# Hedgehog linear attention and an ELU layer on one core: loads by batch, weights in pieces, 64-row tail matmuls, and another order of steps

## The chip, the cores and the metric

One core of one Trainium2 chip. Its engines run their own instruction streams and wait for each other through semaphores: TensorE (PE, matmuls; PEld is its weight load), VectorE (DVE), ScalarE (ACT), GpSimd (POOL), and SyncE (SP), which only issues transfers. POOL issues transfers too: those go on a queue that software fills (`q0 software_dynamic`) and can change the type on the way; SyncE's queue (`q1 hardware_dynamic`) copies as it is. The metric is the device time of one launch in microseconds.

## What is computed

Inputs: q, k, v of shape (batch 8, heads 8, rows 576, 64), w_phi (64, 128), moe_w_in (512, 2048), moe_w_out (2048, 512), all float32; the output is (4608, 512) float32.

```python
def phi(x):
    proj = np.einsum('bhsd,df->bhsf', x, w_phi)
    proj = proj - np.max(np.abs(proj), axis=-1, keepdims=True)
    return np.concatenate([np.exp(proj), np.exp(-proj)], axis=-1)
q_p, k_p = phi(q), phi(k)
kv = np.einsum('bhsf,bhsd->bhfd', k_p, v)
z = np.sum(k_p, axis=2)
num = np.einsum('bhsf,bhfd->bhsd', q_p, kv)
den = np.einsum('bhsf,bhf->bhs', q_p, z)[..., None] + 1e-06
x = (num / den) put back to (4608, 512): a row per token, heads side by side
h = x @ w_in
g = np.where(h > 0.0, h, np.exp(np.minimum(h, 0.0)) - 1.0)
out = g @ w_out
```

## The kernel before

**Quads.** The attention runs in 16 *quads* of four heads, two per batch (`attention_steps`, L154). A head has 576 rows: 512 *main* rows, four to a partition, and a *tail* of 64 rows. Two heads share a 128-row transpose, so a quad has eight main tiles and one tail tile, in which partitions 0 to 63 hold the tails of the even heads (s = 0) and 64 to 127 those of the odd heads (s = 1).

The steps of a quad: `transposes` brings k and q into the layout that the projections need (L166, L174; evicted by VectorE). `k_head` (five: four heads and the tails) projects (L195), takes the maximum of absolute values on VectorE (L202) and two exponentials on ScalarE (L215) into EK. The maximum isn't subtracted: `k_scale` forms exp(-m) and exp(m) (em, L223) and multiplies them into v on POOL (vs, L229, and the tails vst, L240); a column of ones beside v gives z. `q_head` does projection and maximum for q; `q_features` makes the projection the other way round (L250) with its exponentials (L258); `kv` sums EK against vs (L288 tails, L299 main); `out_head` multiplies the features of q with kv (L322) and joins the two halves on VectorE (L331, L337), `out_tail` does so for the tails (L344 to L360); `divide` takes 1/den on VectorE (L367 to L373) and multiplies on POOL (x, L376 and L382); `x_out` transposes x (L393, L405) into xT, the input of the second part.

**MoE units.** Tokens come in nine chunks of 512: chunk b holds the main rows of batch b, the ninth all tails. A first-product unit `mm1(ch, jt)` is four matmuls (L438), an exponential on ScalarE (e_sb), a subtraction on POOL (u_sb, L448) and the select on VectorE (gT, L451); a chunk has 16. A second-product unit `mm2(ch, tt)` is sixteen matmuls (L459), a copy on ScalarE and a store from SyncE; a chunk has four. That makes 180 units.

**Order.** Slot n (n = 0 to 16) holds kv, out and x of quad n-1 and transposes of quad n+1 beside the projections of quad n, by a list written out in `slot_steps` (L483). In the list the transposes of x (`old["x"]`) stand after the q heads and before the q features. Between the steps come MoE units: chunk b is released after slot 2b+2 and its 20 units are spread over the next two slots (L534 to L557); 136 units are placed in slots 3 to 16, 44 follow. The text's order is not quite the order on the engines: the framework plans each engine's stream with costs of its own and may move an instruction ahead of others that it expects to wait.

**Loads.** k and q go through POOL's queue, cast to bf16, per quad (`load_quad`, L131); the tails per batch in six transfers (`load_tails`, L104) into tiles that keep all batches; v through SyncE, one transfer a head, into rows of 65 floats that hold the column of ones. w_in comes in eight transfers before slot 0, w_out in four after slot 1. All PSUM tiles of the attention share four buffers, those of the MoE four others.

Of the kernel before, what the change touches and what calls it, by code (L numbers as in the profile page):

```python
# [8 lines left out]
FP32 = mybir.dt.float32  # L9
# [3 lines left out]
ACT = mybir.ActivationFunctionType  # L13

# [7 lines left out]
def kernel(  # L22
# [10 lines left out]
    nc = tc.nc  # L33
# [12 lines left out]
    N_CHUNK = NTOK // CHUNK  # L46
    NT = 4
    MAIN = NT * P
# [5 lines left out]
    loads = ctx.enter_context(tc.tile_pool(name="loads", bufs=3))  # L54
    work = ctx.enter_context(tc.tile_pool(name="work", bufs=2))
    small = ctx.enter_context(tc.tile_pool(name="small", bufs=4))
    xtp = ctx.enter_context(tc.tile_pool(name="xtp", bufs=3))
# [10 lines left out]
    make_identity(nc, ident)  # L68

    w_phi_both = consts.tile([P, 2, F], BF16)  # L70
    nc.vector.memset(w_phi_both, 0.0)
    nc.gpsimd.dma_start(out=w_phi_both[0:D, 0, :], in_=w_phi)
    nc.gpsimd.dma_start(out=w_phi_both[D:P, 1, :], in_=w_phi)
# [7 lines left out]
    def load_w_in():  # L81
        for ct in range(N_CT):
            for c in range(2):
                nc.gpsimd.dma_start(
                    out=w_in_sb[c * D:(c + 1) * D, ct, :],
                    in_=w_in_r[ct // 2, c, ct % 2],
                )

    def load_w_out():
        for jt in range(0, N_JT, 4):  # L90
            nc.gpsimd.dma_start(
                out=w_out_sb[:, jt:jt + 4, :], in_=w_out_r[:, jt:jt + 4, :]
            )
# [5 lines left out]
    q_tails = consts.tile([P, NQ, 2, D], BF16)  # L99
    k_tails = consts.tile([P, NQ, 2, D], BF16)  # L100
    v_tails = consts.tile([P, NQ, 2, D1], BF16)
    nc.vector.memset(v_tails[:, :, :, D:D1], 1.0)

    def load_tails(b):  # L104
        for src, dst in ((k, k_tails), (q, q_tails), (v, v_tails)):
            heads = src[b].rearrange("(gc s) j d -> s j gc d", s=2)
            for s in range(2):
                nc.gpsimd.dma_start(
                    out=dst[s * TAIL:(s + 1) * TAIL, 2 * b:2 * b + 2, :, 0:D].rearrange(
                        "p g c d -> p (g c) d"  # L110
                    ),
                    in_=heads[s, MAIN:S],
                )


    NV = 3
    v_bufs = []
    for i in range(NV):
        vb = consts.tile([P, 4, NT, D1], FP32, name=f"v_main{i}")
        nc.vector.memset(vb[:, :, :, D:D1], 1.0)  # L120
        v_bufs.append(vb)

    vst_bufs = []
    for i in range(2):
        t = consts.tile([P, 2, 2, 2, D1], BF16, name=f"vst{i}")
        nc.vector.memset(t, 0.0)
        vst_bufs.append(t)

    qk_loaded = {}

    def load_quad(i):  # L131
        b, qd = divmod(i, 2)
        got = []
        for src, nm in ((k, "k_main"), (q, "q_main")):
            t = loads.tile([P, 4, NT * D], BF16, name=nm)
            nc.gpsimd.dma_start(  # L136
                out=t,
                in_=src[b, 4 * qd:4 * qd + 4, 0:MAIN, :].rearrange(
                    "h (p t) d -> p h (t d)", t=NT
                ),  # L140
            )
            got.append(t)
        vb = v_bufs[i % NV]
        for hh in range(4):
            nc.sync.dma_start(
                out=vb[:, hh, :, 0:D],
                in_=v[b, 4 * qd + hh, 0:MAIN, :].rearrange(
                    "(p t) d -> p t d", t=NT
                ),
            )  # L150
        qk_loaded[i] = (got[0], got[1], vb)


    def attention_steps(i):  # L154
# [3 lines left out]
        def transposes():  # L158
            k_main, q_main, _ = qk_loaded[i]
            kT = work.tile([P, 9, P], BF16, name="kT")  # L160
            qT = work.tile([P, 9, P], BF16, name="qT")
            for src, dst in ((k_main, kT), (q_main, qT)):
                tr = apsum.tile([P, 8, P], BF16, name="tr", tag="ap")
                for hh in range(4):
                    for tp in range(2):
                        nc.tensor.transpose(  # L166
                            tr[:, 2 * hh + tp, :],
                            src[:, hh, tp * P:(tp + 1) * P],
                            ident,
                        )  # L170
                nc.vector.tensor_copy(dst[:, 0:8, :], tr)  # L171
            trt = apsum.tile([P, 2, P], BF16, name="trt", tag="ap")
            for n, (src, dst) in enumerate(((k_tails, kT), (q_tails, qT))):
                nc.tensor.transpose(  # L174
                    trt[:, n, :],
                    src[:, i, :, :].rearrange("p c d -> p (c d)"),
                    ident,
                )
            nc.vector.tensor_copy(kT[:, 8, :], trt[:, 0, :])
            nc.vector.tensor_copy(qT[:, 8, :], trt[:, 1, :])  # L180
            st["kT"], st["qT"] = kT, qT
            st["m_k"] = small.tile([P, 18], FP32, name="m_k")
            st["m_q"] = small.tile([P, 18], FP32, name="m_q")
            st["EK"] = work.tile([P, 4, 2, NT * F], BF16, name="EK")
            st["EKt"] = work.tile([P, 2, 2 * F], BF16, name="EKt")
            st["Eq"] = work.tile([P, 2, 2, 2, 4 * P], BF16, name="Eq")
            st["Eqt"] = work.tile([P, 2, 2 * P], BF16, name="Eqt")

        def project(xT, hh, m):
# [4 lines left out]
            for j in range(n):  # L194
                nc.tensor.matmul(  # L195
                    pk[:, 2 * j:2 * j + 2, :].rearrange("p a b -> p (a b)"),
                    xT[:, 2 * hh + j, :],
                    w_phi_rhs,
                    start=True,
                    stop=True,  # L200
                )
            nc.vector.tensor_reduce(  # L202
                m[:, 4 * hh:4 * hh + 2 * n],
# [16 lines left out]
        def k_scale():  # L220
            em = small.tile([P, 2, 18], FP32, name="em")
# [4 lines left out]
            vb = qk_loaded[i][2]  # L226
            vs = work.tile([P, 4, 2, NT, D1], BF16, name="vs")
            for hh in range(4):
                nc.gpsimd.tensor_tensor(  # L229
                    vs[:, hh],  # L230
                    vb[:, hh:hh + 1].to_broadcast((P, 2, NT, D1)),
                    em[:, :, 4 * hh:4 * hh + 4, None].to_broadcast(
                        (P, 2, NT, D1)
                    ),
                    op=ALU.mult,
                )
            vst = vst_bufs[i % 2]
            for s in range(2):
                r = slice(s * TAIL, (s + 1) * TAIL)
                nc.gpsimd.tensor_tensor(  # L240
                    vst[r, :, :, s, :],
                    v_tails[r, i:i + 1].to_broadcast((TAIL, 2, 2, D1)),
                    em[r, :, 16:18, None].to_broadcast((TAIL, 2, 2, D1)),
                    op=ALU.mult,
                )
# [209 lines left out]
    def mm2(ch, tt):  # L455
# [15 lines left out]
        else:  # L471
            for e in range(2):
# [4 lines left out]
                )  # L477

    def slot_steps(n):  # L483
# [104 lines left out]
```

## Time and profile before

| | us |
|---|---|
| median of 3 runs (lowest, highest) | 509.34 (508.05, 510.24) |
| the profiled execution | 507.1 |
| its span in the trace | 505.3 |
| TensorE busy | 409.6 |
| VectorE, POOL, ScalarE busy | 306.1, 278.5, 268.3 |

The span is from the first to the last instruction in the trace. A busy share is an average over stages with different limits; rows of the profile name line, engine, operation, output <- input, shape and count, then busy time and mean length, then the idle time just before and what ended it.

### The profile page before, as it was taken

How to read it: one execution, taken by the hardware profiler on the slowest of the kernel's cores; microseconds unless marked ns; L12 is line 12 of the kernel's file. 1: busy time of each engine (PE TensorE's matmuls, PEld its weight loads, DVE VectorE, ACT ScalarE, POOL GpSimd, SP SyncE). 2: the span in 40 equal slices, each digit the busy share in tenths (PEclk: the TensorE clock that was granted, in tenths of full speed). 3: DMA queues.
4: the chain of work that ended last, by engine and by line, in shares of the span. 5: the costliest groups of instructions: out<-in, count | busy, mean ns of one | idle time of the engine just before them, and what ended most of it. 6: DMA issues, size and time to landing. Idle time of an engine off the chain costs nothing.

```text
span 505.3 us, 8410 instructions
## 1 busy us (share of the span) xinstructions
PE 409.6 (81%) x3070; PEld 223.1 (44%) x3120; DVE 306.1 (61%) x647; ACT 268.3 (53%) x581; POOL 278.5 (55%) x420
## 2 busy tenths in 40 slices
PE   2573727495979797979797979797979798999996
PEld 1251415252635364536363546354545354444442
DVE  2562826886857677766777577757775855334420
ACT  1742608292847474847484748474847462444431
POOL 8669799747473737373737383818281734333310
PEclk9965959797989899989999999999998999899999
DMA  9999948231323232324242424200000000110113
GB/s 157 212 181 198 116 61 76 47 43 43 44 63 64 62 64 64 64 64 64 64 64 62 64 65 64 62 22 21 22 23 23 21 22 22 42 43 21 43 52 72
DMA packets 71944, 32.55 MB, mean 64 GB/s; under 512 B 48352, under 2 KB 66784, under 8 KB 71904
## 3 DMA queue, kind: packets, MB, share of 16 engines
q0 software_dynamic: 32864, 14.19, 23.1%
q1 hardware_dynamic: 39040, 17.83, 13.2%
q8 instruction: 24, 0.39, 0.3%
q14 instruction: 16, 0.13, 0.1%
HBM read 36.77 MB, written 9.44 MB: 91 GB/s over the span
## 4 chain that ended last, share of the span: by engine, by line
PE 52%; POOL 20%; DVE 13%; DMA 6%; issue 4%; ACT 4%; POOLq 0%; ACTq 0%
PE po L459 22%; PE ph L438 13%; POOL x L376 7%; DMA q_main<-in_q_dram 5%; POOL vs L229 4%; DVE m_q L202 4%; PE pq L250 4%; PE pn L322 3%; PE pkv L299 2%; POOL vst L240 2%; PE pk L195 2%; ACT EK L215 2%; POOL u_sb L448 2%; PE tr L166 2%; DVE den L367 2%
## 5 line engine op out<-in xcount | busy, mean ns | idle before, releaser
L448 POOL TENSOR_SCALAR u_sb<-e_sb 128x512 bf16<-128x512 f32 x144 | 88.9, 623 | 134.9 <-ACT e_sb L446 129.5
L459 PE MATMUL po<-w_out_sb,gT 128*128 128x512 bf16 x559 | 148.1, 389 | 1.8 <-DVE gT L451 1.4
L451 DVE SCALAR_TENSOR_TENSOR gT<-u_sb,ph 128x512 bf16<-128x512 bf16 x144 | 97.9, 683 | 78.9 <-POOL u_sb L448 78.1
L438 PE MATMUL ph<-xT,w_in_sb 128*128 128x512 bf16 x480 | 131.0, 390 | 4.6 <-DVE gT L451 3.4
L446 ACT ACTIVATE e_sb<-ph 128x512 f32<-128x512 f32 x144 | 87.3, 611 | 48.8 <-PE ph L438 46.8
L258 ACT ACTIVATE Eq<-pq 128x512 bf16<-128x512 f32 x128 | 65.2, 616 | 54.7 <-PE pq L250 54.7
L459 PEld LDWEIGHTS <-gT 128*128 128x128 bf16 x576 | 54.4, 100 | 50.5 <-issue 4.6
L438 PEld LDWEIGHTS <-w_in_sb 128*128 128x128 bf16 x576 | 54.6, 100 | 49.6 <-issue 6.8
L215 ACT ACTIVATE EK<-pk 128x512 bf16<-128x512 f32 x128 | 69.4, 612 | 13.1 <-DVE m_k L202 13.0
L229 POOL TENSOR_TENSOR vs<-v_main,em 128x520 bf16<-128x520 f32 x64 | 65.7, 1063 | 17.9 <-ACT em L223 17.7
L202 DVE TENSOR_REDUCE m_k<-pk 128x4 f32<-128x512 f32 (+1 forms) x80 | 50.4, 632 | 25.9 <-PE pk L195 25.6
L467 ACT COPY o_sb<-po 128x512 f32<-128x512 f32 x36 | 21.2, 589 | 68.0 <-PE po L459 67.5
L393 PE MATMUL tr<-ident,x 128*128 128x128 bf16 x128 | 14.6, 248 | 52.7 <-POOL x L376 52.7
L202 DVE TENSOR_REDUCE m_q<-pk 128x4 f32<-128x512 f32 (+1 forms) x80 | 48.5, 628 | 1.3 <-PE pk L195 0.5
L322 PEld LDWEIGHTS <-Eq 128*128 128x128 bf16 x512 | 28.9, 98 | 24.9 <-issue 17.0
L376 POOL TENSOR_TENSOR x<-tot,rec 128x256 bf16<-128x256 f32 x64 | 37.2, 614 | 3.1 <-DVE rec L373 3.0
L393 PEld LDWEIGHTS <-x 128*128 128x128 bf16 x128 | 8.4, 108 | 68.8 <-POOL x L376 68.8
L322 PE MATMUL pn<-kv,Eq 128*128 128x65 bf16 x512 | 34.0, 194 | 3.8 <-ACT EK L215 2.6
L195 PE MATMUL pk<-w_phi_both,qT 128*128 128x256 bf16 x144 | 29.6, 292 | 8.4 <-DVE m_q L202 7.0
L136 POOL DMA_DIRECT2D k_main<-in_k_dram x16 | 12.8, 802 | 35.9 <-PE tr L166 25.3
L195 PE MATMUL pk<-w_phi_both,kT 128*128 128x256 bf16 x144 | 29.6, 284 | 3.3 <-ACT EK L215 1.0
L171 DVE COPY kT<-tr 128x1024 bf16<-128x1024 bf16 x16 | 11.1, 692 | 34.1 <-PE tr L166 34.1
(61 smaller groups left out, 462.2 us busy)
## 6 DMA issues: line engine op xcount, KB each, us to landing
v_main<-in_v_dram SPq DMA_DIRECT2D x64, 128.0 KB, 3.3
out_dram<-o_sb SPq DMA_DIRECT2D x32, 256.0 KB, 2.6
k_main<-in_k_dram POOLq DMA_DIRECT2D x16, 256.0 KB, 5.3
q_main<-in_q_dram POOLq DMA_DIRECT2D x16, 256.0 KB, 5.7
w_in_sb<-in_moe_w_in_dram POOLq DMA_DIRECT2D x8, 256.0 KB, 10.2
w_out_sb<-in_moe_w_out_dram POOLq DMA_DIRECT2D x4, 512.0 KB, 8.3
out_dram<-o_sb SPq DMA_DIRECT2D x8, 128.0 KB, 2.3
k_tails<-in_k_dram POOLq DMA_DIRECT2D x16, 32.0 KB, 2.8
```

Source lines behind the costliest of these rows:

```text
L195: nc.tensor.matmul(pk[:, 2 * j:2 * j + 2, :].rearrange("p a b -> p (a b)"), xT[:, 2 * hh + j, :], w_phi_rhs, start=True, stop=True,)
L202: nc.vector.tensor_reduce(m[:, 4 * hh:4 * hh + 2 * n], pk[:, 0:2 * n, :], axis=AX.X, op=ALU.max, apply_absolute_value=True,)
L215: nc.scalar.activation(dst, pk, ACT.Exp, scale=1.0 - 2.0 * sg)
L229: nc.gpsimd.tensor_tensor(vs[:, hh], vb[:, hh:hh + 1].to_broadcast((P, 2, NT, D1)), em[:, :, 4 * hh:4 * hh + 4, None].to_broadcast((P, 2, ...
L258: nc.scalar.activation(st["Eq"][:, par, c, sg, :], pq, ACT.Exp, scale=1.0 - 2.0 * sg)
L322: nc.tensor.matmul(pt[:, t, :], st["Eq"][:, par, c, sg, o:o + P], st["kv"][:, c, s, sg, :], start=True, stop=True,)
L376: nc.gpsimd.tensor_tensor(st["x"][:, s, :, c, :], st["tot"][:, hh, :, 0:D], rec[:, 4 * hh:4 * hh + 4, None].to_broadcast((P, NT, D)), op=A ...
L438: nc.tensor.matmul(ph, w_in_sb[:, ct, jt * P:(jt + 1) * P], xTs[ch][:, ct, :], start=(ct == 0), stop=(ct == N_CT - 1),)
L446: nc.scalar.activation(e_sb, ph, ACT.Exp)
L448: nc.gpsimd.tensor_scalar(u_sb, e_sb, -1.0, 1.0, op0=ALU.add, op1=ALU.mult)
L451: nc.vector.scalar_tensor_tensor(gTs[ch][:, jt, :], u_sb, 0.0, ph, op0=ALU.min, op1=ALU.max)
L459: nc.tensor.matmul(po, gT[:, jt, tt * P:(tt + 1) * P], w_out_sb[:, jt, :], start=(jt == 0), stop=(jt == N_JT - 1),)
```

## The change

- **Loads.** One tile a batch and tensor holds mains and tails (`stage`, two buffers). k and q go by batch in one main and two tail transfers each on POOL's queue (batch 0 by halves), v on SyncE, float32 and contiguous by 1 KB pieces, w_phi on SyncE with a cast on VectorE. There is no column of ones in v: a POOL copy puts em into vs.
- **Weights.** w_in in eight and w_out in eight transfers, issued one after each step of slots 0 and 1, with batch 1's k and q between them. v of batch 1 waits for a memset that stands behind `k_scale` of quad 0.
- **Layout.** The 18 columns of a quad are kept as two heads of nine, so that main and tail share one tile: vs in four products of 128 x 512 and two of 128 x 128, x in two of 128 x 576, and one `den`.
- **Tail matmuls.** `kv` now takes one s at a time and its tails as four matmuls over 64 partitions (rows r); `out_tail` as eight with 64 weight columns into one PSUM tile.
- **Order.** In a slot `x_out` stands last, after q features and transposes; `k_scale` stands before the last two out heads, and q heads between these. Slot 2 does quad 1's kv, out and x first. MoE units run by a rate, 136 over slots 2.5 to 17, and first products are preferred until four have run.

```diff
     def load_main(eng, n, b, h0, h1):
+        eng.dma_start(
+            out=kqv[b][n][:, h0 * HW:h1 * HW].rearrange("p (h n) -> p h n", n=HW),
+            in_=(k, q, v)[n][b, h0:h1, 0:MAIN, :].rearrange(
+                "h (p t) d -> p h (t d)", t=NT
...
         def k_scale():
-            for hh in range(4):
+            vs = st["vs"] = work.tile([P, 2, 2 * NS, D1], BF16, name="vs")
+            nc.gpsimd.tensor_copy(vs[:, :, :, D], em)
+            for c in range(2):
+                for sg in range(2):
+                    r = slice(c * NS, c * NS + 2 * NT)
+                    o = (4 * qd + 2 * c) * HW
+                    nc.gpsimd.tensor_tensor(
+                        vs[:, sg, r, 0:D],
+                        vb[:, o:o + 2 * HW].rearrange("p (n d) -> p n d", d=D),
+                        em[:, sg, r, None].to_broadcast((P, 2 * NT, D)),
...
+        def kv(s):
...
+            r = slice(s * TAIL, (s + 1) * TAIL)
+            for c in range(2):
+                for sg in range(2):
+                    nc.tensor.matmul(
+                        pkv[:, c, sg, :],
+                        st["EKt"][r, sg, c * F:(c + 1) * F],
+                        st["vs"][r, sg, c * NS + 8, :],
...
         def out_tail():
+            pt = apsum.tile([P, 2, 2, D1], FP32, name="pnt", tag="ap")
             for s in range(2):
                 r = slice(s * TAIL, (s + 1) * TAIL)
+                for sg in range(2):
+                    for c in range(2):
+                        o = c * P + s * TAIL
+                        nc.tensor.matmul(
+                            pt[r, sg, c, :],
+                            st["Eqt"][:, sg, o:o + TAIL],
+                            st["kv"][:, s, c, sg, :],
...
+    def moe_unit():
+        if second and (not first or run[0] >= N_JT // 4):
+            mm2(*second.pop(0))
+            run[0] = 0
+            return
+        ch, jt = first.pop(0)
+        mm1(ch, jt)
+        run[0] += 1
+        if jt == N_JT - 1:
+            second.extend((ch, tt) for tt in range(CHUNK // P))
...
+        if n == 2:
+            return (
+                old["kv"] + old["out"] + old["x"]
+                + [lambda: chunk_ready(0)]
+                + new["k"] + new["scale"] + new["q"] + new["qf"] + nxt["tr"]
+            )
...
+        steps = (
+            old["kv"][:1] + kk[:1] + old["kv"][1:] + kk[1:3]
+            + old["out"][:1] + kk[3:4] + old["out"][1:2] + kk[4:]
+            + (new or none)["scale"]
+            + old["out"][2:3] + qq[:1] + old["out"][3:4] + qq[1:2]
+            + old["out"][4:] + qq[2:] + (new or none)["qf"]
+        )
+        if nxt:
+            steps += nxt["tr"]
+        steps += old["x"]
+        if n % 2 == 0:
+            steps.append(lambda: chunk_ready(n // 2 - 1))
...
+    def load_v(b, gate=False):
+        if gate:
+            nc.vector.memset(kqv[b][2][:, 0:1], 0.0)
+        load_main(nc.sync, 2, b, 0, 8)
+        load_tails(nc.sync, 2, b)
...
+    UNITS = 136
...
+        if n % 2 == 0 and 1 < n // 2 + 1 < B:
+            alloc_batch(n // 2 + 1)
+            extra += load_kq(n // 2 + 1)
+            load_v(n // 2 + 1)
         steps = slot_steps(n)
         for j, step in enumerate(steps):
             step()
+            if n == 0 and step is quads[0]["scale"][0]:
+                load_v(1, gate=True)
+            if extra and (n < 2 or j % 3 == 2):
+                extra.pop(0)()
+            due = (n + (j + 1) / len(steps) - 2.5) * UNITS / 14.5
+            while done < due and (first or second):
+                moe_unit()
```

Also, `xtp` has two buffers for three, and `o_sb` two for four.

More of the change, by code (lines that the diff above doesn't have):

```diff
@@ L45 @@
     CHUNK = 512
-    N_CHUNK = NTOK // CHUNK
     NT = 4
+    NS = 9
     MAIN = NT * P
@@ L116 @@
[L116 to L139, printed above, removed]
+    HW = NT * D
@@ L156, in attention_steps @@
         st = {}
[L158 to L187, printed above, removed]
```

369 lines of the change are left out of this document (166 added, 203 removed).

## The prediction

> **What bounds the kernel now.** I began with the page's busy shares and slices.
>
> ```profile
> PE 409.6 (81%) x3070; PEld 223.1 (44%) x3120; DVE 306.1 (61%) x647; ACT 268.3 (53%) x581; POOL 278.5 (55%) x420
> PE   2573727495979797979797979797979798999996
> ...
> PE 52%; POOL 20%; DVE 13%; DMA 6%; issue 4%; ACT 4%; POOLq 0%; ACTq 0%
> PE po L459 22%; PE ph L438 13%; POOL x L376 7%; DMA q_main<-in_q_dram 5%; POOL vs L229 4%; DVE m_q L202 4%; PE pq L250 4%; PE pn L322 3%; PE pkv L299 2%; POOL vst L240 2%; PE pk L195 2%; ACT EK L215 2%; POOL u_sb L448 2%; PE tr L166 2%; DVE den L367 2%
> ```
>
> The average misleads: TensorE is slack in the first fifth, alternates 9 and 7 in the middle and is full at the end. In the chain of waits TensorE has half, but POOL's x and vs come next. So I cut the span where the key transposes of a slot end, and asked for the busy time of each stretch: slots 0, 1 and 2, then slots 6 to 15 in one, slot 16, and what follows it (columns: start:end, length, then busy us of PE, PEld, DVE, ACT, POOL, the granted clock, DMA share, GB/s).
>
> ```profile
> 0.00:21.90 21.90, 10.12 (x60) 6.09 (x60) 9.47 (x22) 9.76 (x21) 15.28 (x29) 1.00 1.15 180
> 21.90:51.70 29.80, 14.85 (x120) 9.34 (x120) 12.15 (x30) 10.58 (x27) 24.45 (x35) 0.60 1.27 192
> 51.70:78.40 26.70, 13.72 (x131) 8.39 (x130) 12.81 (x31) 10.53 (x25) 23.61 (x36) 0.68 0.85 81
> ...
> 152.50:410.00 257.50, 229.09 (x1831) 126.85 (x1860) 181.01 (x389) 159.36 (x350) 138.69 (x204) 0.97 0.24 50
> 410.00:429.60 19.60, 17.13 (x143) 9.17 (x145) 11.67 (x26) 7.37 (x16) 7.63 (x13) 1.00 0.07 28
> 429.60:505.30 75.70, 70.62 (x315) 31.67 (x319) 22.11 (x34) 26.71 (x45) 19.77 (x32) 0.97 0.14 46
> ```
>
> Slots 1 and 2 hold no MoE matmuls worth the name, yet take 29.8 and 26.7 us with POOL busy 24. Ten later slots take 25.75 us each, TensorE busy 22.91 of them (VectorE 18.1, ScalarE 15.9, POOL 13.9). What ends TensorE's idle 2.84 us there is nearly one thing (view of waits for TensorE, 152.5 to 410 us: total us, times, longest):
>
> ```profile
> PE tr L393 <- POOL x L376: 24.6, 20, 2.8
> ```
>
> 2.46 us a slot: the transposes of x stand ahead of the q features, and POOL delivers x late. The middle is TensorE plus one wait. The start is another matter. POOL in order of time (start, length, engine, line; in brackets the idle time before it and what ended it):
>
> ```profile
> 20.20 0.76 POOL L136 DMA_DIRECT2D q_main<-in_q_dram  x1 [0.61 <-DMA w_in_sb<-in_moe_w_in_dram]
> 20.97 4.09 POOL L229 TENSOR_TENSOR vs<-v_main,em 128x520 bf16<-128x520 f32 x4
> 25.04 1.31 POOL L240 TENSOR_TENSOR vst<-v_tails,em 64x260 bf16<-64x260 bf16 x2
> ...
> 34.64 0.75 POOL L91 DMA_DIRECT2D w_out_sb<-in_moe_w_out_dram  x1 [1.50 <-DMA k_main<-in_k_dram]
> 38.44 4.09 POOL L229 TENSOR_TENSOR vs<-v_main,em 128x520 bf16<-128x520 f32 x4
> ```
>
> ```profile
> 11.51 1.44 PE L195 MATMUL pk<-w_phi_both,kT 128*128 128x256 bf16 x6
> ...
> 26.39 0.38 PE L288 MATMUL pkv<-vst,EKt 128*128 128x130 bf16 x2 [4.39 <-POOL vst L240]
> 46.42 1.18 PE L393 MATMUL tr<-ident,x 128*128 128x128 bf16 x8 [8.44 <-POOL x L376]
> ```
>
> POOL issues loads between its products and stops at some of them until an earlier transfer has landed; counted in order of issue, it is each time the one eight before. The work behind then reaches TensorE late: 4.39 and 8.44 us. The order of issue is the planner's, not the text's: the tail loads, written after slots 0 to 12, are all out by 88 us.
>
> ```profile
> L108 POOL DMA_DIRECT2D v_tails<-in_v_dram x16: 610/642/689, 7.4 to 88.0; - x16
> ```
>
> **The change, part by part.** *x last.* The 2.46 us go if POOL's x is done in time. The new slot has 26 steps, scale is the 10th and x the 26th, so in a slot of 23 us 14.2 us lie between. POOL's work in them:
>
> ```profile
> L229 POOL TENSOR_TENSOR vs<-v_main,em 128x520 bf16<-128x520 f32 x64 | 65.7, 1063 | 17.9 <-ACT em L223 17.7
> L376 POOL TENSOR_TENSOR x<-tot,rec 128x256 bf16<-128x256 f32 x64 | 37.2, 614 | 3.1 <-DVE rec L373 3.0
> L382 POOL TENSOR_TENSOR xt<-tott,rec 128x128 bf16<-128x128 f32 x16 | 6.4, 397 | 0.0
> L448 POOL TENSOR_SCALAR u_sb<-e_sb 128x512 bf16<-128x512 f32 x144 | 88.9, 623 | 134.9 <-ACT e_sb L446 129.5
> ```
>
> vs: four of 512 elements at 1.05, two of 128 at 0.40, a short copy at about 0.2 us, 5.2 (now 4 x 1.06 and two vst at 0.62, 5.5). x: from 128 and 256 elements (0.40, 0.61) 1.7 ns an element, so 576 take 1.16, twice, 2.3 (now 2.85). Five u_sb, 3.1. That is 10.6 of 14.2 us; the wait goes, with 3.6 us in hand. What is late next: the q heads and features lean on VectorE and ScalarE without the pause in which these catch up. With 0.612 us an exponential and 0.686 a maximum, I cut the new slot at scale and at the first feature. ScalarE is longest in the first part (ten exponentials of k, kv copies, 2.9 of e_sb: 8.7 us), VectorE in the second (two out heads, tail, five maxima, 2.3 gT: 7.9), ScalarE in the third (7.8): 24.4 us if nothing overlaps across the cuts, against TensorE's own 22. Four PSUM buffers carry work across; I take 0.8 us back per slot.
>
> ```profile
> L215 ACT ACTIVATE EK<-pk 128x512 bf16<-128x512 f32 x128 | 69.4, 612 | 13.1 <-DVE m_k L202 13.0
> L202 DVE TENSOR_REDUCE m_k<-pk 128x4 f32<-128x512 f32 x64 | 43.8, 686 | 25.8 <-PE pk L195 25.6
> ```
>
> *MoE units.* Three pieces of the chain of slot 10 (start, length, matmuls):
>
> ```profile
> 254.83 1.94 PE po L459 x9
> 256.78 0.12 PE pkv L288 x2
> 256.89 0.52 PE pkv L299 x16
> ```
>
> A MoE matmul costs 0.216 us, one of 130 columns 0.06, one of 65 columns 0.033. The same 136 of 180 run before the last x, but over 14.5 slots instead of 14 from slot 3, 9.38 a slot, not 10. A unit averages 1.38 us (16 first products of four matmuls, 4 second ones of sixteen), so a slot loses 0.86. Slot: 25.75 - 2.46 - 0.86 + 0.8 = **23.2 us** (22.4 to 24.4). A new chunk is ready only at the end of an even slot, so units run out before the end of slots 4, 6 and 8 by 3.4, 2.2 and 1.0; they follow in a burst, when the other engines are rested: nothing.
>
> *Tails.* kv has eight matmuls of 64 rows and 65 columns for four of 128 x 130, the output tail eight of 64 weight columns for four. No 64-row matmul is in this trace; the nearest are those of 65 columns:
>
> ```profile
> L299 PE MATMUL pkv<-vs,EK 128*128 128x65 bf16 x512 | 22.5, 197 | 0.0
> L299 PEld LDWEIGHTS <-EK 128*128 128x128 bf16 x512 | 20.4, 100 | 0.0
> ```
>
> In a stream, 16 x 0.033 - 8 x 0.06 = nothing, which I take, since these rows have the same columns. Above: each alone at its recorded length, 16 x 0.197 - 0.48 = +2.7 us a slot. Below nothing they hardly go: 16 instructions replace 8. VectorE loses two of four tail operations and one den per quad, POOL two of six tail issues a batch (0.65 each), and two mains of eight heads (0.76 to twice that) replace four: off the path.
>
> The Trainium skill ("TensorEngine Tiling (Array Packing)", Key Properties) says that changing the tiling mode drains TensorE, and under Performance Considerations that column tiling turns fast weight load off; no run here shows either. Its case is the first rival.
>
> *Loads.* Sizes and times to landing of an issue:
>
> ```profile
> v_main<-in_v_dram SPq DMA_DIRECT2D x64, 128.0 KB, 3.3
> ...
> k_main<-in_k_dram POOLq DMA_DIRECT2D x16, 256.0 KB, 5.3
> ...
> w_in_sb<-in_moe_w_in_dram POOLq DMA_DIRECT2D x8, 256.0 KB, 10.2
> ```
>
> v goes in 1 KB pieces on SyncE's queue, w_phi there too, and POOL has 30 loads to issue until w_out is out. The first projection (11.51) now waits for q's transposes too; k alone is transposed and copied by about 9, so em is ready near 15, not 17.6. vs of quad 0 can start there, or behind as many issues as now (21), or behind all 30, when the 22nd has landed: 5.6 MB (k, q, v of batch 0, w_in, k and q of batch 1) at the 186 GB/s of the first two stretches, 30 us, 36 with v of batch 1 between. I take 19, so kv starts at 24.0 (20 to 40), not 26.4. Slot 1 then lasts 25.3 (26.4 to 51.7) less the 8.44 us wait, 17: 41, by when batch 1 is in. Slot 2 does the old quad and its x first, unhidden (kv and out 6, x with its products 4, 10 us), then the new quad's 11 us (slot 0 from its first projection) and some four MoE units, 5 us: 26, ending at 67 where it now ends at 78.4. SyncE's wait for a free v buffer has only stores behind it, two a slot, and o_sb has two buffers; the buffer of batch b+2 was read out a slot before: nothing, and if a store did wait a whole slot, one second product.
>
> **Sum.** 67 + 13 x 23.2 (slots 3 to 15) + 18.7 (slot 16, 19.6 less 0.86; its x wait stays) + 75.7 (the same 44 units) = 463.0 span; with the 1.8 us around the span, 464.8 against the profiled execution's 507.1. The median of the runs shown is 2.2 above that execution: **467**.
>
> **Rivals.** (1) *Each change of tiling mode drains TensorE*: six a quad (into and out of two kv tails and the output tail), each 0.197 less 0.033, 1.0 us, 14 slots, +14: 481. For it: a matmul's recorded length is 0.164 us more than its place in a stream; against: matmuls of three shapes already follow each other at 33 to 60 ns here. 13%. (2) *The wait on x stays*, since POOL is late by issuing loads and because slot 16 and slot 2 show how x directly behind its products costs: S = 24.9, 13 x 1.7 = +22: 489. Against: 3.6 us in hand. 14%. (3) *The loads go ahead of vs for quads 0 and 1*, so slots 0 to 2 take 78 as now: +11, 478. For it: the planner has pulled loads forward already. 9%. (4) **Slower**: the weights of the 64-row and 64-column tails load with nothing over them, and each matmul then runs alone, 0.100 + 0.197 for 16, less 0.48: +4.3 a quad, 14 slots, +60: 527. It decides from +3.0 a quad, 0.19 us a matmul. For it: such a row is unknown here; against: TensorE loads weights under other matmuls throughout (PEld 44% inside PE's 81%). 12%, 2 of them inside the 0.5% that this kernel's timing can tell from no change.
>
> **The chances.** The forecast has 52%, with 452 to 481 as its own range (S from 22.4 to 24, kv from 20 to 30). Rivals 1 to 3 are all faster: 88 in all. Slower 10, same 2. For 8 in 10 I go from 450 (6% below) to 492, which leaves rival 4 and a little of 2 above.
>
> **What would show it.** Right: TensorE's wait on x under 8 us in all, mostly slots 2 and 16; slots of about 23 us with TensorE over 93% busy; slot 2 over by about 67; the first MoE matmul near 55. Wrong: tail matmuls (kv and pnt) with gaps of 0.1 us or more around them (rivals 1, 4); x still the largest wait (2); TensorE waiting for vs beyond 30 us (3); or ScalarE as the releaser of most idle time, S near 24.4.

## The result, and the profile after

The changed kernel takes **473.13 us** (median of 4 runs, 469.91 to 474.40) beside 508.83 us for the kernel before on the same chip; the ratio is 0.9286 with an interval of 0.9234 to 0.9338. The forecast was 467, its range 450 to 492. The profiled execution took 472.63 us with a span of 470.9.

The page of the changed kernel, busy shares, slices and chain:

```profile
PE 406.8 (86%) x3248; PEld 224.3 (48%) x3248; DVE 279.0 (59%) x596; ACT 262.6 (56%) x581; POOL 247.7 (53%) x360
...
PE   1674687899989998999898979799869898999995
...
PE 51%; POOL 20%; ACT 11%; DVE 8%; issue 5%; DMA 4%; POOLq 0%; ACTq 0%
PE po L407 23%; PE ph L386 13%; POOL vs L192 7%; ACT EK L174 5%; POOL u_sb L396 4%; DMA q_b<-in_q_dram 4%; POOL x L331 3%; PE pkv L250 3%; DVE gT L399 3%; PE pk L153 3%; ACT e_sb L394 3%; ACT Eq L217 2%; PE tr L133 2%; POOL vs L200 2%; PE tr L341 2%
```

In the middle, 9 and 8 with a few 7s and a 6 stand where 9 and 7 alternated; x fell in the chain from 7% to 3%, and VectorE from 13% to 8%. POOL still holds 20%, but now with vs ahead of everything else that it does.

The same kernel cut into stretches: from 24 us, where kv of quad 0 was forecast to start, slot 1 until its key transposes end, the stall behind them, the rest of slot 2, slots 3 to 15, slot 16, and what follows (start:end, length, busy us of PE, PEld, DVE, ACT and POOL, clock, DMA share, GB/s):

```profile
24.00:41.00 17.00, 12.75 (x125) 8.51 (x123) 11.60 (x27) 10.76 (x27) 13.18 (x21) 0.70 1.09 157
41.00:50.00 9.00, 2.58 (x33) 2.28 (x33) 1.93 (x6) 1.57 (x5) 9.00 (x13) 0.75 1.20 233
50.00:77.50 27.50, 18.99 (x151) 10.99 (x149) 13.50 (x32) 13.13 (x31) 13.78 (x20) 0.81 0.45 66
77.50:381.20 303.70, 279.81 (x2443) 158.23 (x2441) 210.78 (x461) 195.52 (x446) 172.85 (x245) 0.98 0.29 59
381.20:397.90 16.70, 15.19 (x147) 8.23 (x145) 9.64 (x22) 6.81 (x14) 7.09 (x10) 1.00 0.09 33
397.90:470.90 73.00, 68.14 (x316) 30.72 (x314) 23.30 (x36) 26.12 (x44) 19.72 (x32) 0.98 0.15 44
```

Set against the stretches of before, the 34.4 us of span come from few places:

| stretch | before | forecast | after |
|---|---|---|---|
| to the end of slot 2 | 78.4 | 67 | 77.5 |
| slots 3 to 15, in all | 331.6 (78.4 to 410.0) | 301.6 | 303.7 |
| one of these slots | 25.5 | 23.2 | 23.36 |
| slot 16 | 19.6 | 18.7 | 16.7 |
| what follows | 75.7 | 75.7 | 73.0 |
| span | 505.3 | 463.0 | 470.9 |

The middle gave 27.9 us where the forecast has 30.0. The start gave 0.9 instead of 11.4. TensorE's waits over the whole span (total us, times, longest) and, in order of time, the two transposes of x that lie in the start:

```profile
PE tr L341 <- POOL x L331: 11.8, 5, 6.2
PE ph L386 <- DVE gT L399: 11.6, 9, 3.5
...
PE po L407 <- DVE gT L399: 4.2, 2, 2.3
```

```profile
48.30 1.03 PE L341 MATMUL tr<-ident,x 128*128 128x128 bf16 x8 [6.24 <-POOL x L331]
...
59.10 1.03 PE L341 MATMUL tr<-ident,x 128*128 128x128 bf16 x8 [3.46 <-POOL x L331]
```

Of the 11.8 us on x, 6.24 and 3.46 lie in slots 1 and 2. In the middle x is no longer waited for: 0.6 us in slots 3 to 15, where the kernel before has

```profile
PE tr L393 <- POOL x L376: 32.2, 23, 5.3
```

The largest wait there is now on gT, the output of the ELU: 12.3 us of its 11.6 + 4.2 = 15.8.

### The profile page after: what moved, and what is told of

Same layout as the page of the kernel before. It is cut to its first block, busy times and chain, and to the rows that moved or that the text cites. A ratio compares the mean times of both kernels' runs of the same rounds, so it can differ in the third digit from the quotient of the medians.

```text
span 470.9 us, 8519 instructions
## 1 busy us (share of the span) xinstructions
PE 406.8 (86%) x3248; PEld 224.3 (48%) x3248; DVE 279.0 (59%) x596; ACT 262.6 (56%) x581; POOL 247.7 (53%) x360
## 4 chain that ended last, share of the span: by engine, by line
PE 51%; POOL 20%; ACT 11%; DVE 8%; issue 5%; DMA 4%; POOLq 0%; ACTq 0%
PE po L407 23%; PE ph L386 13%; POOL vs L192 7%; ACT EK L174 5%; POOL u_sb L396 4%; DMA q_b<-in_q_dram 4%; POOL x L331 3%; PE pkv L250 3%; DVE gT L399 3%; PE pk L153 3%; ACT e_sb L394 3%; ACT Eq L217 2%; PE tr L133 2%; POOL vs L200 2%; PE tr L341 2%
## 5 line engine op out<-in xcount | busy, mean ns | idle before, releaser
L396 POOL TENSOR_SCALAR u_sb<-e_sb 128x512 bf16<-128x512 f32 x144 | 87.3, 617 | 129.9 <-ACT e_sb L394 120.9
L386 PE MATMUL ph<-xT,w_in_sb 128*128 128x512 bf16 x512 | 139.9, 386 | 12.0 <-DVE gT L399 11.6
L407 PE MATMUL po<-w_out_sb,gT 128*128 128x512 bf16 x576 | 139.7, 383 | 4.2 <-DVE gT L399 4.2
L174 ACT ACTIVATE EK<-pk 128x512 bf16<-128x512 f32 x128 | 67.9, 624 | 26.7 <-DVE m_k L161 26.3
L386 PEld LDWEIGHTS <-w_in_sb 128*128 128x128 bf16 x576 | 52.2, 98 | 58.5 <-issue 20.3
L192 POOL TENSOR_TENSOR vs<-v_b,em 128x512 bf16<-128x512 f32 x64 | 65.3, 1043 | 17.5 <-ACT em L182 17.4
L331 POOL TENSOR_TENSOR x<-tot,rec 128x576 bf16<-128x576 f32 x32 | 36.0, 1146 | 15.7 <-DVE rec L328 15.6
L293 DVE TENSOR_TENSOR tot<-pn,w 128x260 f32<-128x260 f32 x64 | 27.0, 422 | 10.4 <-PE pn L283 10.2
L209 PE MATMUL pq<-qT,w_phi_both 128*128 128x512 bf16 x64 | 22.8, 421 | 4.9 <-DVE m_q L161 2.8
L299 DVE TENSOR_TENSOR tot<-tot,pn 128x260 f32<-128x260 f32 x64 | 26.6, 417 | 0.4
## 6 DMA issues: line engine op xcount, KB each, us to landing
w_in_sb<-in_moe_w_in_dram POOLq DMA_DIRECT2D x8, 256.0 KB, 12.4
```

The source lines that it names most:

```text
L174: nc.scalar.activation(dst, pk, ACT.Exp, scale=1.0 - 2.0 * sg)
L192: nc.gpsimd.tensor_tensor(vs[:, sg, r, 0:D], vb[:, o:o + 2 * HW].rearrange("p (n d) -> p n d", d=D), em[:, sg, r, None].to_broadcast((P, 2 ...
L331: nc.gpsimd.tensor_tensor(st["x"][:, :, c, :], st["tot"][:, r, 0:D], rec[:, r, None].to_broadcast((P, NS, D)), op=ALU.mult,)
L386: nc.tensor.matmul(ph, w_in_sb[:, ct, jt * P:(jt + 1) * P], xTs[ch][:, ct, :], start=(ct == 0), stop=(ct == N_CT - 1),)
L396: nc.gpsimd.tensor_scalar(u_sb, e_sb, -1.0, 1.0, op0=ALU.add, op1=ALU.mult)
L407: nc.tensor.matmul(po, gT[:, jt, tt * P:(tt + 1) * P], w_out_sb[:, jt, :], start=(jt == 0), stop=(jt == N_JT - 1),)
```

## The experiments

All eleven kernels were timed in three rounds beside the kernel before. The change's own ratio has an interval of 0.0052 to each side, some 2.6 us, so a median that lies less than 3 us from 473.13 isn't told apart from it by time alone.

### Is it the place of x?

**x last, alone** (b_xlast), in the kernel before:

```diff
         steps += qs
-        if old:
-            steps += old["x"]
         if new:
             steps += new["qf"]
             quads[n] = new
         if n + 1 < NQ:
             steps.append(lambda: transpose_next(n + 1))
+        if old:
+            steps += old["x"]
```

> The kernel before with one part of the change alone: x_out stands after the q features and the transposes of the next quad, loads, tails, layout and MoE pacing as before. Theory A (the wait on x is what the change wins): TensorE's wait on x falls from 52.7 us in all to under 10 and about 0.9 us a slot comes back elsewhere, so 509 - 43 + 12 = about 478 us, nearly all of the gain. Rival B (loads, layout and pacing are needed for the gain): the wait goes but slots 1 to 4 stay behind POOL's tail loads, 490 us or more.

**All of the change but that** (a_xmid), in the changed kernel:

```diff
-            + old["out"][4:] + qq[2:] + (new or none)["qf"]
+            + old["out"][4:] + qq[2:] + old["x"] + (new or none)["qf"]
         )
         if nxt:
             steps += nxt["tr"]
-        steps += old["x"]
```

> The changed kernel with x_out put back ahead of the q features in slots 3 to 15 (slots 1 and 2 too where the list has it), all else as changed. Theory A: the wait of about 2.4 us a slot returns over 13 slots and the 0.9 us that had come back goes, so 473 + 20 = 493 us or more (up to 505). Rival B: under 485 us, since the new loads and layout bring x early enough anyway.

x last alone gives 478.96 us, ratio 0.943 (0.9393 to 0.9468): 29.0 us less than before. The change without it gives 499.59 us, 0.9844 (0.981 to 0.9878): 8.4 us less, which is within 2%. The sum is 37.4 beside the 35.7 of the whole, so the two are nearly independent. TensorE's waits, first of the kernel before with x last, then of the change without it:

```profile
PE pq L250 <- DVE m_q L202: 15.2, 19, 1.7
PE tr L393 <- POOL x L376: 12.3, 4, 6.9
```

```profile
PE tr L341 <- POOL x L331: 37.5, 15, 13.4
PE ph L386 <- DVE gT L399: 16.7, 15, 3.2
```

In the second, 25.7 us more of waiting on x (37.5 less 11.8) answer to 26.5 us of time. The wait on gT stands there too: 16.7 us and another 4.3 ahead of the second products, 21.0 in all, more than the 15.8 of the changed kernel; the kernel before has 3.4 + 1.4. So it isn't the new place of x that brought the wait on gT, but the rest of the change; which part of it, no run separates. For the first, the same row of the kernel before:

```profile
PE tr L393 <- POOL x L376: 52.7, 27, 9.7
```

x falls by 40.4 us and the time by 29.0, so 11.4 are given back, 0.8 a slot over 14 slots. The largest wait is now that of the q projections on the maxima, which VectorE still forms. Eight slots of this kernel, 7 to 14:

```profile
162.44:355.28 192.84, 176.64 (x1472) 100.35 (x1496) 143.71 (x313) 124.67 (x280) 110.88 (x164) 1.00 0.27 56
```

That is 24.1 us a slot, where the forecast's two terms for x give 25.75 - 2.46 + 0.8 = 24.09. Here the give-back is as the forecast had it, in size and on VectorE. In the changed kernel the largest wait of these slots is another.

### What is late next in the middle

The chain of waits of the changed kernel in one slot (start, length, what):

```profile
323.86 2.87 POOL vs L192 x3
...
327.46 0.59 POOL u_sb L396
328.08 0.69 DVE gT L399
...
329.02 2.26 POOL x L331 x2
331.28 0.59 POOL u_sb L396
```

A u_sb of 0.59 us comes after the vs block, and the next after both products of x. The MoE unit that needs it then lacks gT. I tested this, and its rival (TensorE itself is the bound), four ways.

**More for TensorE** (a_pnt3): each matmul of the output tail is issued three times, with the same result.

```diff
-                        nc.tensor.matmul(
+                        for _ in range(3):
+                            nc.tensor.matmul(
...
```

> The changed kernel with each of the eight output tail matmuls with 64 weight columns done three times in place (same result), 16 more a quad. Theory (TensorE sets the length of the slots, and such a matmul costs 0.033 us as in a stream): 0.53 us in each of 13 or 14 slots, +6 to +8 us, 479 to 481. Rival of the drain (0.15 us or more each): +25 us or more. Rival (the waits on VectorE and POOL set the slots, TensorE has room): within 2 of 473.

It takes 473.74 us, 0.9322 (0.93 to 0.9344). The theory that TensorE's time is the slot's time falls: some 0.5 us more a quad cost nothing that can be told. In order of time, TensorE about one such tail of this kernel, then about three tails of the changed one:

```profile
200.51 0.85 PE L309 MATMUL pnt<-kv,Eqt 128*64 128x65 bf16 x24
201.29 0.39 PE L153 MATMUL pk<-w_phi_both,qT 128*128 128x256 bf16 x2
```

```profile
215.31 0.20 PE L262 MATMUL pkv<-vs,EKt 64*128 64x65 bf16 x1
215.44 0.60 PE L386 MATMUL ph<-xT,w_in_sb 128*128 128x512 bf16 x2
...
324.43 0.38 PE L153 MATMUL pk<-w_phi_both,qT 128*128 128x256 bf16 x2
324.74 0.33 PE L308 MATMUL pnt<-kv,Eqt 128*64 128x65 bf16 x8
325.00 0.39 PE L153 MATMUL pk<-w_phi_both,qT 128*128 128x256 bf16 x2
325.23 1.03 PE L386 MATMUL ph<-xT,w_in_sb 128*128 128x512 bf16 x4
...
382.94 0.67 PE L250 MATMUL pkv<-vs,EK 128*128 128x65 bf16 x16
383.54 0.29 PE L262 MATMUL pkv<-vs,EKt 64*128 64x65 bf16 x4
383.77 1.04 PE L386 MATMUL ph<-xT,w_in_sb 128*128 128x512 bf16 x4
```

From start to start a matmul with 64 weight columns takes 0.26 / 8 = 0.0325 us, and in the longer row 0.78 / 24 = 0.0325 too: nothing is lost on leaving these. On entering there is a pause: two matmuls of 256 columns take 0.31 us ahead of the tail and 0.23 behind it (0.08 more), and sixteen of 65 columns take 0.60 ahead of the 64-row tail, where the prediction's pieces of the kernel before show 0.52 (0.08 more). One matmul of 64 rows takes 0.13 us until the next other one starts, four take 0.23: 0.033 each, and 0.10 once on leaving.

**No subtraction** (a_no_usb): u_sb is left out, and gT reads e_sb instead, so the - 1 of the ELU is missing.

```diff
-        u_sb = moesm.tile([P, CHUNK], BF16, name="u_sb")
-        nc.gpsimd.tensor_scalar(
-            u_sb, e_sb, -1.0, 1.0, op0=ALU.add, op1=ALU.mult
-        )
         nc.vector.scalar_tensor_tensor(
-            gTs[ch][:, jt, :], u_sb, 0.0, ph, op0=ALU.min, op1=ALU.max
+            gTs[ch][:, jt, :], e_sb, 0.0, ph, op0=ALU.min, op1=ALU.max
```

> The changed kernel with the subtraction u_sb on POOL left out: VectorE's select reads e_sb directly, so the part g of the computation lacks its - 1 where h is negative. Theory (POOL is the late one: vs in a block stands ahead of u_sb, gT and the PSUM buffers behind it): TensorE's wait on gT goes and the time falls by at least the 7 us of a_vs_split, to 466 or less, 460 if TensorE's idle time in slots 3 to 15 (24 us of 304) halves. Rival (VectorE and ScalarE set the slots): 470 or more.

444.31 us, 0.874 (0.8709 to 0.8772), 28.8 less than the change. Twelve slots, 4 to 15, of this kernel and then of the changed one:

```profile
89.70:352.00 262.30, 252.75 (x2239) 146.44 (x2277) 193.49 (x425) 180.71 (x412) 103.65 (x132) 1.00 0.29 61
```

```profile
97.00:380.70 283.70, 261.78 (x2274) 147.57 (x2275) 192.70 (x424) 180.75 (x411) 157.22 (x222) 0.98 0.27 56
```

262.3 / 12 = 21.86 us a slot beside 23.64, with TensorE busy 96% of it. So without u_sb on POOL, with POOL busy only 55% of these slots, each is 1.8 us shorter. Of the 21.4 us, 12.4 are idle time of TensorE (21.92 to 9.55); the other 9.0 are busy time, at a granted clock of 1.00 beside 0.98 and with 35 fewer matmul records, and whether u_sb has a part in them isn't shown. Nor does the run tell the place of u_sb in POOL's line from the hop itself: gT now starts straight after e_sb.

**vs in pieces** (a_vs_split): each of its products, until then one block in `k_scale`, goes behind one of the steps that follow.

```diff
+        if new:
+            for m, f in enumerate(new["vs"]):
+                steps[10 + m] = both(steps[10 + m], f)
...
```

> The changed kernel with the products vs no longer written in one block after em: one product of 512 elements, then the two of the tail, behind each of the five steps after k_scale. Theory (u_sb stands up to 5 us behind the run of vs on POOL, gT comes late and TensorE waits 11 to 16 us in all on gT): the wait on gT falls under 6 us and the time by 4 to 9 us, 464 to 469. Rival (POOL's order is the planner's, or x and kv come later for it): 473 within 2 or slower.

465.92 us, 0.9165 (0.9141 to 0.919). The time is as expected, the wait is not: it stands at 12.4 us (9.0 and 3.4) where I had expected less than 6. The twelve slots take 279.7 us, 4.0 less than in the change, and the span ahead of them gives the rest. TensorE's wait ahead of the first products:

```profile
PE ph L393 <- DVE gT L406: 9.0, 11, 2.2
```

The block is part of the price, the smaller one (4.0 us beside the 21.4 of a_no_usb in the same slots). The waits are shorter now (2.2 us at most, not 3.5) and more in number: POOL still does u_sb behind something else.

**u_sb on VectorE** (a_usb_dve), on top of the best version (below):

```diff
-        nc.gpsimd.tensor_scalar(
+        nc.vector.tensor_scalar(
             u_sb, e_sb, -1.0, 1.0, op0=ALU.add, op1=ALU.mult
```

> The kernel of a_best with the subtraction u_sb on VectorE instead of POOL, same result. Theory (what costs in the slots is that u_sb queues on POOL behind vs and x, not the work as such): TensorE's wait on gT goes and the time falls by half or more of what leaving u_sb out gave in the slots (28), to 430 to 445. Rival (VectorE, 62% busy, becomes the late engine with 144 more operations of 0.4 to 0.6 us): 455 or more.

464.54 us, 0.9112 (0.9056 to 0.9168): 6.5 us more than the same kernel with u_sb on POOL. The gain that I had expected doesn't come, and the time is the rival's. Below stand TensorE's largest wait, then u_sb in this kernel (shortest, median and longest in ns, first and last start), then two of them in order of time with what POOL does meanwhile:

```profile
PE ph L396 <- DVE gT L409: 13.1, 19, 4.1
```

```profile
L406 DVE TENSOR_SCALAR u_sb<-e_sb x144: 354/420/3631, 56.4 to 445.2; 128x512 bf16<-128x512 f32 x144
```

```profile
84.83 2.08 DVE L406 TENSOR_SCALAR u_sb<-e_sb 128x512 bf16<-128x512 f32 x2
```

```profile
84.18 2.44 POOL L339 TENSOR_TENSOR x<-tot,rec 128x576 bf16<-128x576 f32 x2 [1.53 <-DVE rec L336]
```

The instruction is shorter on VectorE (0.42 us in the median) than on POOL (0.617), but not while POOL multiplies: the 37 that overlap one of POOL's products vs or x take 0.96 us in the mean, the other 107 take 0.43. u_sb has changed engines and is still held up beside vs and x. It also stands in one line with gT, the maxima and the evictions now, and TensorE waits longer for gT, not shorter: 13.1 + 2.1 us beside 9.0 + 3.4. What a_no_usb took away can't be had by handing the work to VectorE. Which of the two costs the 6.5 us, and what u_sb would cost with nothing ahead of it, the run doesn't show.

### Where the start stays

POOL of the changed kernel in order of time, through slots 0 and 1:

```profile
20.84 0.34 POOL L187 CAST vs<-em 128x36 bf16<-128x36 f32 x1 [6.70 <-ACT em L182]
...
33.16 0.71 POOL L83 DMA_DIRECT2D w_out_sb<-in_moe_w_out_dram  x1 [0.71 <-DMA w_in_sb<-in_moe_w_in_dram]
35.61 2.11 POOL L83 DMA_DIRECT2D w_out_sb<-in_moe_w_out_dram  x3 [1.74 <-DMA k_b<-in_k_dram]
39.00 2.13 POOL L83 DMA_DIRECT2D w_out_sb<-in_moe_w_out_dram  x3 [1.28 <-DMA q_b<-in_q_dram]
41.10 0.38 POOL L187 CAST vs<-em 128x36 bf16<-128x36 f32 x1
```

ScalarE's em of quad 1, in order of time:

```profile
33.55 0.34 ACT L182 ACTIVATE em<-m_k 128x18 f32<-128x18 f32 x2
```

Three things are late. em of quad 0 is ready at 20.8. vs of quad 1 starts at 41.1, 7.2 us after its em, since POOL issues w_out first and stops three times at the landing of an earlier transfer. x of quad 0 stands behind that vs and starts at 46.00, hence the 6.24 us. Four kernels take them one by one.

**k before q in quad 0** (a_kfirst): the transposes of q come after `k_scale`, so that TensorE doesn't wait for q's transfer first.

```diff
-            return new["k"] + new["scale"] + new["q"] + new["qf"] + nxt["tr"]
+            return (
+                new["k"] + new["scale"] + new["tr"][1:] + new["q"] + new["qf"]
+                + nxt["tr"]
+            )
...
-    for step in quads[0]["tr"]:
-        step()
+    quads[0]["tr"][0]()
```

> The changed kernel; in slot 0 the q transposes stand after k_scale, so that TensorE's k projections don't queue behind q's transfer. Theory (the order on TensorE sets when em of quad 0 is ready): em at about 15.5 instead of 20.4, kv of quad 0 four us earlier, and 2 to 4 us off the time. Rival (q's transfer and the work after it set the end of slot 0 anyway): the ends of slots 0 and 1 and the time stay, 473 within 2.

468.43 us, 0.923 (0.9199 to 0.9261): 4.7 less than the change, where I had expected 2 to 4. The copy of em, first step of vs, starts 6.2 us earlier; the wait on x of quad 0 grows from 6.24 to 8.78, and its transposes start at 45.03, 3.3 earlier. POOL in order of time:

```profile
14.68 0.34 POOL L187 CAST vs<-em 128x36 bf16<-128x36 f32 x1 [1.53 <-ACT em L182]
```

**v of batch 1 behind em** (a_vgate): in the changed kernel the memset that was to hold this load back ran at once, since nothing that it needs comes late: VectorE runs it at 0.95 us. Here a copy of em stands in its place.

```diff
-            nc.vector.memset(kqv[b][2][:, 0:1], 0.0)
+            nc.vector.tensor_copy(kqv[b][2][:, 0:1], ems[0][:, 0, 0:1])
```

> The changed kernel; the main load of v of batch 1 is really held until em of quad 0 exists (a copy of em into its first column instead of the memset, which ran at 0.95 us and held nothing). Theory (1 MB of v beside the first k and q delays q, whose transposes stand ahead of the k projections): q's first half lands near 10 instead of 12.3, em of quad 0 at about 18 instead of 20.4, and the time falls by 1 to 3 us. Rival (w_in takes the bandwidth that v leaves): q lands as late, 473 within 1.5.

470.14 us, 0.9244 (0.9218 to 0.927), not told apart from the change. The load is now issued at 20.57 us. TensorE takes up q's transposes at 12.09 (in the change at 12.27) after 3.32 us of waiting, where I had expected q near 10. The early load of v isn't what makes q late. What does is left open.

**w_out behind em of quad 1** (a_wout_late): its eight issues come after `k_scale` of quad 1, held there by a copy from em into the tile.

```diff
-    extra += [lambda jt=jt: load_w_out(jt) for jt in range(0, N_JT, 2)]
...
+            if n == 1 and step is quads[1]["scale"][0]:
+                nc.vector.tensor_copy(
+                    w_out_sb[:, :, 0], ems[1][:, 0, 0:N_JT]
+                )
+                extra += [lambda jt=jt: load_w_out(jt) for jt in range(0, N_JT, 2)]
```

> The changed kernel; the eight pieces of w_out are issued after k_scale of quad 1, held there by a copy of em of quad 1 into the tile that they overwrite. Theory (POOL's issue of w_out blocks vs of quad 1): vs starts at about 34, when em of quad 1 is ready, instead of 41.1, TensorE's wait of 6.2 us on x of quad 0 goes, and the time falls by 4 to 7 us to 466 to 469. Rival (the transfers themselves set the start): the wait moves to another load, 473 within 2.

467.11 us, 0.92 (0.9174 to 0.9226). vs of quad 1 now starts 8.0 us earlier than in the change, and the wait on x of quad 0 falls to 2.00; but the loads of k and q for batch 2 stop four times at w_out's landing (0.97 to 1.42 us), and x of quad 1 behind them costs 5.88 where it cost 3.46. POOL, then TensorE:

```profile
33.12 0.35 POOL L190 CAST vs<-em 128x36 bf16<-128x36 f32 x1 [0.64 <-ACT em L184]
```

```profile
43.98 1.03 PE L344 MATMUL tr<-ident,x 128*128 128x128 bf16 x8 [2.00 <-POOL x L334]
...
57.03 1.03 PE L344 MATMUL tr<-ident,x 128*128 128x128 bf16 x8 [5.88 <-POOL x L334]
```

**All three, with w_out behind em of quad 2** (a_start4): the edits of the last three, where the third names slot 2 and `ems[2]`; in slot 2, too, a load is then issued after each step.

```diff
+            if n == 2 and step is quads[2]["scale"][0]:
+                nc.vector.tensor_copy(
+                    w_out_sb[:, :, 0], ems[2][:, 0, 0:N_JT]
+                )
...
-            if extra and (n < 2 or j % 3 == 2):
+            if extra and (n < 3 or j % 3 == 2):
```

> The changed kernel with the start mended in three places: q transposes of quad 0 after its k_scale, v of batch 1 held until em of quad 0, w_out held until em of quad 2 (slot 2) so that neither vs of quad 1 nor x of quad 1 stands behind it. Theory (each removes its own wait): slot 2 ends near 65 instead of 77.5 and the time is 460 to 463. Rival (once one wait is gone the transfers bind): 465 to 467, as with one mend alone.

461.57 us, 0.909 (0.9058 to 0.9121), 11.6 less than the change. x of quad 0 is transposed at 36.37, not 48.30, without a wait.

Slots 4 to 15 of this kernel, from the transposes of x to those of x twelve slots on:

```profile
86.15:370.04 283.89, 262.04 (x2278) 147.75 (x2276) 193.20 (x425) 181.46 (x413) 157.26 (x222) 0.98 0.26 55
```

They take 283.9 us, where the change has 283.7, and begin some 11 us earlier. The slots are not faster, so the gain lies ahead of them.

### The best version

**The better start and vs in pieces** (a_best): a_start4 with the edit of a_vs_split.

> Both mends together: the start of a_start4 (q transposes of quad 0 after its k_scale, v of batch 1 and w_out really held) and the vs products one per step as in a_vs_split. Theory (they lie in different stages: a_start4 gained its time before the end of slot 3, a_vs_split most of it after): the gains add, 473 - 11.6 - 7.2 = 454 (452 to 456). Rival (both free the same POOL time): 458 to 461.

458.08 us, 0.9004 (0.8972 to 0.9036): faster than both kernels, 50 us below the one before and 15 below the change. Slots 4 to 15 take 279.6 us, as in a_vs_split, 4.1 less than in the change, and begin 11.7 us earlier.

By the profiled executions the gains nearly add: the span is 455.0, 15.9 below the change's, where a_start4 and a_vs_split alone take off 10.8 and 6.2. By the medians they add less, 15.1 of 18.8; I had expected 452 to 456, and 458.08 lies at the edge of the rival's case, in which they overlap (458 to 461). Whether one or four us are lost between them isn't settled.

## Why the prediction came out as it did

**x last: right, mechanism and size.** 2.46 us a slot were to go, 32.0 over slots 3 to 15, and of the 32.2 of waiting that were there all but 0.6 went; 29.0 us come from this edit alone, and putting x back costs 26.5. Its terms on POOL hold: vs at 1.043 us (forecast 1.05), x at 1.146 (1.16). Rival 2, x still late at 489, is thereby refuted.

**MoE units: the term fails.** They were to save 0.86 us a slot, 11.2 over the 13 slots, because 9.38 would run in a slot instead of 10. The weight loads of the MoE matmuls in slots 3 to 15, first and second products, of the kernel before and then of the changed one (length, busy us of PE and of PEld):

```profile
78.40:410.00 331.60, 102.85 (x377) 37.29 (x402) 0.95 0.26 50
78.40:410.00 331.60, 98.02 (x340) 32.46 (x352) 0.95 0.26 50
```

```profile
77.50:381.20 303.70, 108.30 (x390) 34.25 (x390) 0.98 0.29 59
77.50:381.20 303.70, 93.00 (x368) 34.48 (x368) 0.98 0.29 59
```

402 + 352 = 754 before, 390 + 368 = 758 after: over these slots nothing is saved. I had taken the ten units of slots 6 to 15 for all thirteen. In slots 3 and 4 the kernel before has only the 16 first products of chunk 0, so there the change adds units; slots 3 to 5 have some 57 loads more, slots 6 to 15 some 52 fewer.

**What is late next: right for x alone, wrong for the changed kernel.** I took back 0.8 us a slot for VectorE and ScalarE, whose work no longer fits the cuts. In b_xlast that is what happens, in size and on VectorE. In the changed kernel the waits are on gT behind POOL. I had counted u_sb's 3.1 us only as part of POOL's work ahead of x, where it fits, and not asked who waits for each u_sb as it stands behind vs or x. As a_xmid has this wait too, it belongs to the rest of the change and not to x. That VectorE can't take u_sb over without loss shows in a_usb_dve; whether it is near being the bound itself stays open, as u_sb is held up beside POOL's products there.

**The middle as a sum: near by luck.** With 32.2 us of waiting gone and no units saved, 32.2 - 27.9 = 4.3 us came back over the 13 slots, from whatever cause, where I had 0.8 x 13 = 10.4. And 13 x 25.75 = 334.8 was 3.2 more than the 331.6 that these slots took. So the 11.2 us of saving that did not come were nearly made up by 6.1 us less of give-back and by a starting point 3.2 us lower than I had it: 303.7 instead of 301.6, 23.36 a slot instead of 23.2.

**Tails: nothing in the time, but not free.** The pauses come to 2 x (0.08 + 0.10) + 0.08 = 0.44 us a quad, with the matmuls 16 x 0.033 + 0.44 - 8 x 0.06 = 0.49, where I had 0.05; a_pnt3 shows that TensorE has room for 0.5. Rival 1 (a drain at each change of mode, 1.0 us a quad, 481) had a pause at five of its six changes, at less than half its price, and its 14 us in the time are not seen; how much of the time the pauses take, no run tests. Rival 4 (each matmul alone, 0.297 us, 527) falls: they follow each other at 0.033. The Trainium skill's rule that a change of the tiling mode drains TensorE ("TensorEngine Tiling (Array Packing)", Key Properties) agrees with the pauses of 0.08 to 0.10 us on entering either mode and on leaving the 64 rows; on leaving the 64 columns the trace shows none. The loads of 64 weight columns, for which I had cited the loss of fast weight load (the page has it under Restrictions), are a little longer than those of 128 (112 ns, 100 in the prediction's rows) and hidden.

**The start: the step that failed.** Slot 2, "26, ending at 67", measured 36.5 us and 77.5. kv of quad 0 started at 25.71 (forecast 24.0) and slot 1 ended at 41, as forecast; but I took the 8.44 us wait on x out of slot 1 as gone, when x last in the slot moves it behind the key transposes, which is where I had set the boundary. From 41.0 the changed kernel takes 8.1 us until x of quad 0 is transposed (I had none), 10.9 instead of 10 for the old quad, 17.5 instead of 16 for the new one and its units: together the 10.5 us. a_wout_late shows whose wait it is: eight issues of w_out on POOL, ahead of vs of quad 1. This is the mechanism of rival 3, which I gave 9% and a price of 11; it came true for quad 1 alone, at nearly its whole price: slots 0 to 2 take 77.5 us where it has 78. I left it out of the likeliest case because slot 1 was to end at 41, "by when batch 1 is in". Batch 1 was, but POOL, with w_out to issue, was not free. a_start4 gets 11.6 us back and comes to 461.57; its span of 460.1 is below the 463.0 of the sum. Two smaller errors went unseen behind it: em of quad 0 came near 20.8, not 15, because TensorE took q's transposes first (a_kfirst: 14.68); and then vs started at once, where I had allowed four us of issues.

**Slot 16 and what follows** came out 2.0 and 2.7 us better than forecast. In slot 16 the wait on x, which I had kept as it was, fell from 2.3 us to 1.5, and the slot has ten fewer weight loads of MoE matmuls (55, before 65), some 2.2 us at 0.216 each, where the forecast took off 0.86. In the last stretch 2.5 of the 2.7 us are busy time of TensorE (70.62 to 68.14); it has five fewer weight loads (319 to 314), 1.1 us. What shortened the rest no run shows. These 4.7 us hide part of the start's error: 10.5 + 2.1 (slots) - 2.0 - 2.7 = 7.9, the span's 470.9 less 463.0.

**The number.** 473.13 lies inside the range, 6.1 us from the forecast and 4.9 from rival 3's 478. That it is no farther off is in part luck: the start's 10.5 us were lessened at the end, and the errors of the middle cancelled.

**What was to show it.** Wait on x under 8 us, mostly slots 2 and 16: 11.8, of which 9.7 in slots 1 and 2 and 1.5 in slot 16. TensorE above 93% of a slot: 92% (279.81 / 303.70). Slot 2 over by 67: no. First MoE matmul near 55: 52.30, earlier than forecast, and yet slot 2 was late, so this sign was a poor one: the first two of a unit's four matmuls need x of quad 0 alone, the other two and the slot's end also x of quad 1. Gaps of 0.1 us about the tails, a sign of rivals 1 and 4: 0.08 to 0.10, so that sign did show, without their times.

## What to carry to other kernels

When the order of a slot is rewritten, ask of each engine what else stands behind its long blocks; small instructions there (0.6 us here) can become the next wait, though the engine is half idle. A saving worked out for some slots must be counted over all that it is multiplied by. A stall of the start must be followed through the boundary at which one cuts: an engine that both computes and issues transfers is late by its issues and by the landings at which it stops (here 7.2 us, 3.0 of them at two landings). And a load is held back only by something that depends on late data; an instruction that merely stands later in the text may run at once.

## What the runs showed of the hardware

- Between other matmuls, one of 64 weight columns or of 64 rows (65 columns each) takes 0.033 us. Entering a group of either costs a pause of some 0.08 us and leaving the 64 rows 0.10, some 0.44 us a quad here.
- Work on an engine that is busy 55% of a stretch (POOL, 157.22 of 283.70 us) can still lengthen it: without u_sb a slot of 23.6 us is 1.8 shorter, as a_no_usb shows.
- The subtraction of a 128x512 tile from float32 to bf16 takes 0.617 us on POOL. On VectorE it takes 0.43 us in the mean, and 0.96 where it overlaps a product on POOL (up to 3.63); moving it to VectorE cost 6.5 us.
